# In the expert slots: h copied by DMA, transposed as float32r, and in the middle of the next first product

## The chip, the cores and the metric

The kernel runs on one core of a Trainium2 chip. Its metric is the device time of one execution in microseconds. Before the change the median of three runs is 1048.81 us (1048.38 to 1049.65). One more execution was recorded by the hardware profiler; it took 1047.6 us, and all views below are of it.

## The reference

Three stages in float32: attention with a position bias over 4 × 8 heads, a mixture of experts that sends each of 2304 tokens to one expert of eight, and a dense two-layer part. The change is in the second:

```python
N, D, E, F = (2304, 512, 8, 1024)
e_idx = np.argmax(logits, axis=1)
for e in range(E):
    mask = e_idx == e
    h = np.maximum(x[mask] @ w1[e], 0.0)
    out[mask] = gate_w[mask, None] * (h @ w2[e])
```

The third stage multiplies its (2304, 512) input by (512, 2048), applies `h * 1/(1+exp(-1.702 h))` and multiplies by (2048, 512).

## The kernel before

The attention part ends at about 340 us, the routing follows, the expert slots run from about 365 to 630 us, and the dense part to the end. A tile framework with a scheduler sets the order of the instructions on each engine from the order of the code, the buffers and its own estimates; each engine then works strictly through its queue and waits on semaphores.

Tokens are sorted by expert, and an expert slot is 128 sorted tokens of one expert. 21 slots always run; two more blocks of two stand behind a branch (`optional`, L981 and L982) and are skipped with this data. Products are made of three float32r matmuls, because each operand is split in a high part (a cast on ScalarE, names with h) and a low part (a subtraction on VectorE, names with l): high × high, high × low, low × high (`mm3`). For slot s:

- `gather` brings the 128 rows of x (`xg`), by an indirect DMA from GpSimd's queue. `load_w` brings eight pieces of the expert's weights (`wraw`) by SyncE's queue, only where the expert is new; `split_w` casts each piece on ScalarE (`wh`, L840) and subtracts on VectorE (`wl`, L842). Weight pieces are numbered 8 s to 8 s + 7: four for the first product and four for the second. There are ten buffers for each kind.
- `tx` transposes x with four float32r transposes (`turn`, L146) and splits it into `xh` and `xl` (L861, L862).
- `p1` is the first product, 24 matmuls of 128x512 (L867) in four steps k_ over two halves of h, and two ReLU activations into `h` in SBUF (L882).
- `th` transposes h, eight plain float32 transposes of 128x128 with the identity `ident` (L892), and splits it into `hh` (L894) and `hl` (L895).
- `p2_` is the second product, 24 matmuls (L867), the scaling by the gate into `y` (L908), and a store of `y` to DRAM (`Yc`, L910) from GpSimd's queue.

`run` interleaves them by slots: `p1` of slot s, `tx` of slot s+1, `p2_` of slot s−1, splits of the next weights, `th` of slot s, the rest of the splits. The first slots also carry the end of the routing (small work on all engines).

Beside the slots from 13 on, pieces 4 to 7 of the dense weights are converted in steps that `along` hands out: `conv_load` (L154 to L156) loads a raw piece `cvraw` into one of two buffers, and `conv_steps` works on it: s1 an Abs on ScalarE (L167), s2 to s4 four rows on VectorE (L171 to L181), s5 a cast on ScalarE (L188), s6 a subtraction on VectorE (L194). `conv_list` puts the load of the next piece ahead of the steps of one. The dense part's products are `f` (L1030) and `o` (L1063); the first `f` and `o` groups are worked on around the last slot, and `o` needs the converted pieces.

Of the kernel before, what the change touches and what calls it, by code (L numbers as in the profile page):

```python
# [9 lines left out]
F32 = mybir.dt.float32  # L10
F32R = mybir.dt.float32r
F16 = mybir.dt.float16
I32 = mybir.dt.int32
# [100 lines left out]
def body(ctx, tc, qk, vv, few, mid, ew1, ew2, ww, cst, alog, out, dbg=None):  # L114
    nc = tc.nc
    pe, act, dve, pool, sp = nc.tensor, nc.scalar, nc.vector, nc.gpsimd, nc.sync
# [23 lines left out]
    ident = cs[:, C_ID:C_ID + 128]  # L140
# [3 lines left out]
    def turn(out_, in_):  # L144

        pe.transpose(out_.bitcast(F32R), in_.bitcast(F32R), identr)  # L146
# [3 lines left out]
    wpool = {}  # L150
# [1 line left out]
    P = {}  # L152

    def conv_load(n):  # L154
        raw = wpool["cv"].tile([128, 1024], I32, tag="cvraw", bufs=2, name=f"cvraw{n}")
        sp.dma_start(raw, wwi[n])  # L156
        rw = raw.rearrange("p (n w) -> p n w", w=2)
        P[n] = {"L": rw[:, :, 0], "H": rw[:, :, 1]}

    def conv_steps(n):  # L160

        def s1():
            d = P[n]
            d["a"] = wpool["cv"].tile([128, 512], I32, tag="cva", bufs=1, name=f"cva{n}")
            tc.keep_in_program_order(act.activation(d["a"].bitcast(F32), d["H"].bitcast(F32), AF.Abs))  # L167

        def s2():
            d = P[n]  # L170
            dve.tensor_scalar_max(d["a"].bitcast(F32), d["a"].bitcast(F32), 2.0 ** -15)  # L171
            dve.tensor_scalar(d["a"], d["a"], 5, 2, op0=ALU.logical_shift_left, op1=ALU.logical_shift_right)

        def s3():
            d = P[n]
            dve.scalar_tensor_tensor(d["a"], in0=d["H"], scalar=-1073741824, in1=d["a"],
                                     op0=ALU.bitwise_and, op1=ALU.bitwise_or)

        def s4():
            d = P[n]  # L180
            dve.scalar_tensor_tensor(d["a"], in0=d["L"], scalar=29, in1=d["a"],  # L181
                                     op0=ALU.logical_shift_right, op1=ALU.bitwise_or)

        def s5():
            d = P[n]
            pool_ = wpool["w0"] if n % 12 < 8 else wpool["w1"]
            d["hi"] = pool_.tile([128, 512], F32R, tag=f"wh{n % 12}", name=f"wh{n}")
            act.copy(d["hi"], d["a"].bitcast(F32))  # L188

        def s6():  # L190
            d = P.pop(n)
            pool_ = wpool["w0"] if n % 12 < 8 else wpool["w1"]
            lo = pool_.tile([128, 512], F32R, tag=f"wl{n % 12}", name=f"wl{n}")
            dve.tensor_tensor(lo, d["a"].bitcast(F32), d["hi"].bitcast(F32), op=ALU.subtract)  # L194
            wt[n] = (d["hi"], lo)
        return [s1, s2, s3, s4, s5, s6]

    wwi = ww.bitcast(I32)

    def conv_list(ns, first_loaded=False):  # L200
        out_ = [] if first_loaded else [lambda: conv_load(ns[0])]
        for i, n in enumerate(ns):
            if i + 1 < len(ns):
                out_.append(lambda m=ns[i + 1]: conv_load(m))
            out_ += conv_steps(n)
        return out_
# [597 lines left out]
    def experts():  # L804
        with ExitStack() as cx:
# [5 lines left out]
            raw, wsp, xg, xt, hs, ht = {}, {}, {}, {}, {}, {}  # L811
# [34 lines left out]
            def gather(s_, last):  # L846
                if s_ >= last:
                    return
                t = xg[s_] = mp.tile([128, DM], F32, tag="xg", bufs=3, name=f"xg{s_}")
                V["gather"] = pool.indirect_dma_start(t, None, X, bass.IndirectOffsetOnAxis(ap=rt[:, s_:s_ + 1], axis=0)).ins  # L850
# [18 lines left out]
            def cols(pair, sl):  # L869
                return [t[:, sl] for t in pair]  # L870

            def p1(s_):
                ps = [one(f"p1_{s_}_{f}", "two") for f in range(2)]
                x = xt.pop(s_)
                for k_ in range(4):
                    w = wsp.pop(8 * s_ + k_)
                    a = cols(x, slice(128 * k_, 128 * k_ + 128))
                    for f in range(2):
                        mm3(ps[f], a, cols(w, slice(512 * f, 512 * f + 512)), k_ == 0, k_ == 3)
                h = hs[s_] = m1.tile([128, 1024], F32, tag="h", name=f"h_{s_}")  # L880
                for f in range(2):
                    act.activation(h[:, 512 * f:512 * f + 512], ps[f], AF.Relu)  # L882

            def th(s_):
                h = hs.pop(s_)
                hh = m1.tile([128, 1024], F32R, tag="hh", name=f"hh{s_}")
                hl = m1.tile([128, 1024], F32R, tag="hl", name=f"hl{s_}")
                for f in range(2):
                    ps = one(f"th{s_}_{f}")
                    for k_ in range(4):  # L890
                        c0 = 512 * f + 128 * k_
                        pe.transpose(ps[:, 128 * k_:128 * k_ + 128], h[:, c0:c0 + 128], ident)  # L892
                    sl_ = slice(512 * f, 512 * f + 512)
                    act.copy(hh[:, sl_], ps)  # L894
                    dve.tensor_tensor(hl[:, sl_], ps, hh.bitcast(F32)[:, sl_], op=ALU.subtract)  # L895
                ht[s_] = (hh, hl)
# [15 lines left out]
            def run(first, count, between=()):  # L912

                last = first + count
                gather(first, last)
                gather(first + 1, last)
                for n in range(6):
                    if n == 3:
                        tx(first, last, tc.keep_in_program_order)
                    split_w(8 * first + n, last)  # L920
                for s_ in range(first, last + 1):
                    gather(s_ + 2, last)
                    if s_ < last:
                        p1(s_)
                    with tc.issue_after(V["mm"]) if s_ == first else ExitStack():
                        tx(s_ + 1, last)
                    if s_ - first in between:
                        between[s_ - first]()
                    if s_ > first:
                        p2_(s_ - 1)  # L930
                    for j in range(4):
                        if s_ == first and j >= 2:
                            split_w(8 * s_ + 4 + j, last)
                        split_w(8 * (s_ + 1) + j, last)
                    if s_ < last:
                        th(s_)
                    for j in range(4, 8):
                        split_w(8 * (s_ + 1) + j, last)

# [10 lines left out]
            def rest_of_routing():  # L950
                if not last_steps:
                    last_steps.append(route_last())
                with tc.issue_after(V["gather"]), tc.issue_after(V["split"]):
                    if next(last_steps[0], "end") == "end":
                        rcx.close()

            steps = conv_list([4, 5, 6, 7])

            def along(n, *fs):
# [86 lines left out]
    def dense():  # L1046
        with ExitStack() as cx:
            wpool["w1"] = cx.enter_context(tc.tile_pool(name="w1", bufs=1))
            wpool["cv"] = cx.enter_context(tc.tile_pool(name="cv2", bufs=1))
            d2 = cx.enter_context(tc.tile_pool(name="d2", bufs=2))  # L1050
            dp = cx.enter_context(tc.tile_pool(name="dp", bufs=1))
            po = {}
# [87 lines left out]
```

## Time and profile before

| what | value |
|---|---|
| median of three runs | 1048.81 us (1048.38 to 1049.65) |
| the profiled execution | 1047.6 us, span 1046.0 us |
| PE busy | 997.0 us, 95% of the span |
| DVE busy | 753.9 us, 72% |
| ACT busy | 638.9 us, 61% |
| POOL busy | 133.7 us, 13% |
| weight splits on DVE, L842 | 167 of 1244 ns |
| weight casts on ACT, L840 | 168 of 1064 ns |

The shares are means over the attention, the slots and the dense part, which load the engines differently. A row of a timeline has its start and its duration from the profile; where instructions of one engine are pipelined, the step from one start to the next is what one costs, and it is shorter than the duration.

### The profile page before, as it was taken

What the parts mean: (1) busy time and instruction counts of PE and PEld (TensorE: products, weight loads), DVE (VectorE), ACT (ScalarE), POOL (GpSimd) and SP (SyncE); (2) the same over time, 40 slices, a digit from 0 to 9 for tenths busy, and PEclk for the clock granted to TensorE, in tenths of its full rate; (3) what the DMA queues carried; (4) which work ended last, traced back from release to release, by engine and by line L of the source; (5) the groups of instructions that cost most, each with busy time, mean ns of one, the idle gap of its engine ahead of it and who ended that gap; (6) DMA issues with size and microseconds to landing.
All of it is one profiled execution on the core that took longest, in us unless ns stands there. A gap on an engine that the chain in (4) does not pass through costs nothing. (4 is left out here: it accounts for less than half of the span.)

```text
span 1046.0 us, 16882 instructions
## 1 busy us (share of the span) xinstructions
PE 997.0 (95%) x5806; PEld 817.5 (78%) x5806; DVE 753.9 (72%) x1476; ACT 638.9 (61%) x1203; POOL 133.7 (13%) x136
## 2 busy tenths in 40 slices
PE   5799999999999499999999999999999999999997
PEld 1246777777777378888888888999989999999996
DVE  7786888788788799999999984635563666374433
ACT  7776777687777489999999973544342333232221
POOL 6410000000000344551111000000000000001212
PEclk9899999999999799999999999999999999999999
DMA  8887766776851332511261342400120111010111
GB/s 248 297 239 214 208 170 176 202 208 164 213 143 43 132 108 56 198 41 57 75 232 61 130 133 83 141 31 29 53 81 1 41 61 61 1 41 31 51 41 60
DMA packets 52058, 119.02 MB, mean 114 GB/s; under 512 B 8449, under 2 KB 17921, under 8 KB 51969
## 3 DMA queue, kind: packets, MB, share of 16 engines
q1 hardware_dynamic: 47024, 101.88, 32.9%
q0 software_dynamic: 4800, 15.73, 4.3%
q8 instruction: 47, 0.77, 0.3%
q14 instruction: 43, 0.34, 0.1%
q10 hardware_dynamic: 144, 0.29, 0.1%
HBM read 146.57 MB, written 25.84 MB: 165 GB/s over the span
## 5 line engine op out<-in xcount | busy, mean ns | idle before, releaser
L842 DVE TENSOR_TENSOR wl<-wraw,wh 128x1024 fp32r<-128x1024 f32 x167 | 198.6, 1244 | 6.7 <-ACT wh L840 4.9
L840 ACT CAST wh<-wraw 128x1024 fp32r<-128x1024 f32 x168 | 171.5, 1064 | 18.5 <-DMA wraw<-in_moe_w_dram 8.6
L1033 ACT ACTIVATE sg<-f 128x384 f32<-128x384 f32 x96 | 47.2, 491 | 177.5 <-PE f L1030 177.5
L1035 DVE TENSOR_TENSOR gg<-f,sg 128x384 f32<-128x384 f32 x96 | 53.4, 556 | 139.8 <-ACT sg L1033 139.7
L1030 PE MATMUL f<-yh,wh 128*128 128x384 f32 x384 | 129.9, 338 | 1.0 <-ACTq L982 1.0
L574 DVE CUSTOM_DVE_ANT_0 p<-sc,bias 128x576 f32<-128x576 f32 x144 | 106.3, 752 | 32.4 <-PE sc L571 31.3
L1030 PE MATMUL f<-yh,wl 128*128 128x384 f32 x384 | 129.5, 337 | 0.0
L1030 PE MATMUL f<-yl,wh 128*128 128x384 f32 x384 | 129.5, 337 | 0.0
L578 ACT ACTIVATE p<-p,mx 128x576 f32<-128x576 f32 x144 | 111.3, 774 | 20.0 <-DVE mx L574 16.4
L1063 PE MATMUL o<-wh,gl 128*128 128x512 f32 x288 | 114.0, 396 | 0.0
L1063 PE MATMUL o<-wl,gh 128*128 128x512 f32 x288 | 113.4, 394 | 0.0
L1063 PE MATMUL o<-wh,gh 128*128 128x512 f32 x288 | 113.4, 394 | 0.0
L571 PE MATMUL sc<-kk,qh 128*128 128x288 f32 x320 | 101.3, 334 | 4.1 <-ACT bev L253 1.9
L571 PE MATMUL sc<-kk,ql 128*128 128x288 f32 x320 | 88.8, 296 | 0.0
L1038 ACT CAST gh<-gg 128x384 fp32r<-128x384 f32 x96 | 49.3, 513 | 53.1 <-DVE gg L1035 52.8
L654 PE MATMUL pv<-pt,v 128*64 128x256 f32 (+2 forms) x528 | 77.5, 411 | 0.0
L1030 PEld LDWEIGHTS f<-yh,wh 128*128 128x128 f32 x384 | 72.1, 188 | 5.2 <-ACTq L982 1.4
L1039 DVE TENSOR_TENSOR gl<-gg,gh 128x384 fp32r<-128x384 f32 x96 | 53.5, 557 | 30.7 <-ACT gh L1038 30.7
L1030 PEld LDWEIGHTS f<-yl,wh 128*128 128x128 f32 x384 | 72.1, 188 | 4.1
L599 PE MATMUL tp<-cs,p 128*128 128x128 f32 x512 | 75.0, 274 | 0.2
L1030 PEld LDWEIGHTS f<-yh,wl 128*128 128x128 f32 x384 | 72.1, 188 | 0.0
L571 PEld LDWEIGHTS sc<-kk,qh 128*128 128x128 f32 x320 | 62.9, 197 | 10.4 <-ACT bev L253 3.7
(180 smaller groups left out, 2015.9 us busy)
## 6 DMA issues: line engine op xcount, KB each, us to landing
wraw<-in_moe_w_dram SPq DMA_DIRECT2D x176, 512.0 KB
cvraw<-in_ww_dram SPq DMA_DIRECT2D x32, 512.0 KB
biasD<-bev SPq DMA_DIRECT2D x36, 295.5 KB
raw<-in_qk_dram SPq DMA_DIRECT2D x16, 640.0 KB
Yc<-y POOLq DMA_DIRECT2D x21, 256.0 KB, 2.4
v<-in_vv_dram SPq DMA_DIRECT2D x16, 320.0 KB
kk<-qh SPq DMA_DIRECT2D x16, 320.0 KB
kk<-ql SPq DMA_DIRECT2D x16, 320.0 KB
```

Source lines behind the costliest of these rows:

```text
L571: pe.matmul(ps[:, hf, :288], lhsT=l_, rhs=r_[:, 288 * hf:288 * hf + 288], start=n == 0, stop=n == len(terms) - 1)
L574: dve.tensor_tensor_reduce(out=pp.rearrange("p (a j) -> p a j", a=2), in0=ps[:, :, :288], in1=bt[:, h].rearrange("p (a j) -> p a j", a=2), ...
L578: act.activation(pp, pp, AF.Exp, bias=mx[:, h:h + 1], scale=-1.0, accum_out=rs[:, c % 2, h:h + 1] if c < 4 else rs)
L599: pe.transpose(ps[:, 128 * cc:128 * cc + 128], p[:, c0:c0 + 128], ident)
L654: pe.matmul(ps[64 * h:64 * h + 64, :W], lhsT=vm[g][:, 256 * h + 64 * cc:256 * h + 64 * cc + 64], rhs=G["pt", half][:, 4 * h + cc, cols], s ...
L840: act.copy(h, t)
L842: V["split"] = by.tensor_tensor(l, t, h.bitcast(F32), op=ALU.subtract).ins
L1030: pe.matmul(ps, lhsT=w[x_][:, 128 * k_:128 * k_ + 128], rhs=y_[:, k_, :], start=k_ == 0 and n_ == 0, stop=k_ == 3 and n_ == 2)
L1035: dve.tensor_tensor(gg, ps, sg, op=ALU.mult)
L1038: act.copy(gh, gg)
L1039: dve.tensor_tensor(gl, gg, gh.bitcast(F32), op=ALU.subtract)
L1063: pe.matmul(po[t_], lhsT=a_[:, sl_], rhs=b_, start=fc == 0 and n_ == 0, stop=fc == 3 and n_ == 2)
```

## The change

`p1` gets a function that it calls when two of its four steps are through, and `run` passes one that does `th` of the slot before. `th` is no longer called behind `p2_`. Each half of h, once it is activated, is copied by a DMA from GpSimd's queue into a new tile `hd`, and `th` transposes `hd` by `turn`, as float32r, instead of h. For pieces 4 to 7 of the dense weights `cvraw` has one buffer instead of two, and each load stands directly ahead of its own steps; the dense part has two buffers again.

```diff
     def conv_load(n):
-        raw = wpool["cv"].tile([128, 1024], I32, tag="cvraw", bufs=2, name=f"cvraw{n}")
+        raw = wpool["cv"].tile([128, 1024], I32, tag="cvraw", bufs=wpool.get("cvn", 2), name=f"cvraw{n}")
...
     def conv_list(ns, first_loaded=False):
+        if wpool.get("cvn") == 1:
+            return [f for n in ns for f in [lambda m=n: conv_load(m)] + conv_steps(n)]
         out_ = [] if first_loaded else [lambda: conv_load(ns[0])]
...
-            def p1(s_):
+            def p1(s_, halfway):
                 ps = [one(f"p1_{s_}_{f}", "two") for f in range(2)]
...
                         mm3(ps[f], a, cols(w, slice(512 * f, 512 * f + 512)), k_ == 0, k_ == 3)
-                h = hs[s_] = m1.tile([128, 1024], F32, tag="h", name=f"h_{s_}")
+                    if k_ == 1:
+                        halfway()
+                h = m1.tile([128, 1024], F32, tag="h", name=f"h_{s_}")
+
+                hd = hs[s_] = m1.tile([128, 1024], F32, tag="hd", name=f"hd_{s_}")
                 for f in range(2):
                     act.activation(h[:, 512 * f:512 * f + 512], ps[f], AF.Relu)
+                    pool.dma_start(hd[:, 512 * f:512 * f + 512], h[:, 512 * f:512 * f + 512])
...
-                        pe.transpose(ps[:, 128 * k_:128 * k_ + 128], h[:, c0:c0 + 128], ident)
+                        turn(ps[:, 128 * k_:128 * k_ + 128], h[:, c0:c0 + 128])
...
+                    def halfway():
+                        if s_ > first:
+                            th(s_ - 1)
                     if s_ < last:
-                        p1(s_)
+                        p1(s_, halfway)
+                    else:
+                        halfway()
...
-                    if s_ < last:
-                        th(s_)
...
+            wpool["cvn"] = 1
             steps = conv_list([4, 5, 6, 7])
...
+            wpool["cvn"] = 2
             d2 = cx.enter_context(tc.tile_pool(name="d2", bufs=2))
```

On TensorE, in a settled slot, the transposes of slot 3's h (`th3_0` and `th3_1`) stood between the second product of slot 2 and the first product of slot 4:

```order
L867 MATMUL p2_2_5233<-wh_23_5022,hh2_5154 128x512
L867 MATMUL p2_2_5233<-wl_23_5023,hh2_5154 128x512
L867 MATMUL p2_2_5233<-wh_23_5022,hl2_5155 128x512
L892 MATMUL th3_0_5310<-cs_75,h_3_5218 128x128 x4
L892 MATMUL th3_1_5317<-cs_75,h_3_5218 128x128 x4
L867 MATMUL p1_4_0_5346<-wh_32_5270,xh4_5226 128x512
L867 MATMUL p1_4_0_5346<-wl_32_5271,xh4_5226 128x512
```

In the changed kernel, at the same place of TensorE's queue, they stand in the middle of slot 4's first product and read `hd_3`:

```order
L869 MATMUL p1_4_1_5343<-wh_33_5305,xh4_5238 128x512
L869 MATMUL p1_4_1_5343<-wl_33_5306,xh4_5238 128x512
L869 MATMUL p1_4_1_5343<-wh_33_5305,xl4_5239 128x512
L146 MATMUL th3_0_5358<-identr_77,hd_3_5228 128x128 x4
L146 MATMUL th3_1_5365<-identr_77,hd_3_5228 128x128 x4
L869 MATMUL p1_4_0_5342<-wh_34_5310,xh4_5238 128x512
L869 MATMUL p1_4_0_5342<-wl_34_5311,xh4_5238 128x512
```

The transposes moved behind half a product, with the same neighbours otherwise.

On VectorE, at the first slots, the low part of slot 0's h (`hl0`) stood behind slot 1's x and ahead of the splits of slot 1's weights (`wl_8` to `wl_15`) and of a late one of slot 0 (`wl_6`):

```order
L862 TENSOR_TENSOR xl1_4740<-tx1_4734,xh1_4739 128x512
L895 TENSOR_TENSOR hl0_4817<-th0_0_4818,hh0_4816 128x512
L895 TENSOR_TENSOR hl0_4817<-th0_1_4825,hh0_4816 128x512
L842 TENSOR_TENSOR wl_8_4769<-wraw0_4596,wh_8_4768 128x1024
L842 TENSOR_TENSOR wl_9_4792<-wraw1_4597,wh_9_4791 128x1024
L842 TENSOR_TENSOR wl_6_4797<-wraw6_4602,wh_6_4796 128x1024
L842 TENSOR_TENSOR wl_10_4802<-wraw2_4598,wh_10_4801 128x1024
L842 TENSOR_TENSOR wl_11_4812<-wraw3_4599,wh_11_4811 128x1024
L842 TENSOR_TENSOR wl_12_4833<-wraw4_4600,wh_12_4832 128x1024
L842 TENSOR_TENSOR wl_13_4838<-wraw5_4601,wh_13_4837 128x1024
L842 TENSOR_TENSOR wl_14_4843<-wraw6_4602,wh_14_4842 128x1024
L842 TENSOR_TENSOR wl_15_4848<-wraw7_4603,wh_15_4847 128x1024
```

On the same engine in the changed kernel:

```order
L864 TENSOR_TENSOR xl1_4743<-tx1_4737,xh1_4742 128x512
L844 TENSOR_TENSOR wl_8_4772<-wraw0_4596,wh_8_4771 128x1024
L844 TENSOR_TENSOR wl_9_4795<-wraw1_4597,wh_9_4794 128x1024
L844 TENSOR_TENSOR wl_6_4800<-wraw6_4602,wh_6_4799 128x1024
L844 TENSOR_TENSOR wl_10_4805<-wraw2_4598,wh_10_4804 128x1024
L844 TENSOR_TENSOR wl_11_4815<-wraw3_4599,wh_11_4814 128x1024
L844 TENSOR_TENSOR wl_12_4820<-wraw4_4600,wh_12_4819 128x1024
L844 TENSOR_TENSOR wl_13_4825<-wraw5_4601,wh_13_4824 128x1024
L844 TENSOR_TENSOR wl_14_4830<-wraw6_4602,wh_14_4829 128x1024
L844 TENSOR_TENSOR wl_15_4835<-wraw7_4603,wh_15_4834 128x1024
L902 TENSOR_TENSOR hl0_4856<-th0_0_4857,hh0_4855 128x512
L902 TENSOR_TENSOR hl0_4856<-th0_1_4864,hh0_4855 128x512
```

The two rows of `hl0` moved from ahead of the nine splits to behind them; in later slots, too, hl stands behind the eight splits of the next slot's weights.

On ScalarE at the join, ahead of the branch (`COMPARE_AND_BRANCH`), piece 7 of the dense weights had its Abs (`cva7`) and its cast (`wh7`) ahead of the last slot's result `y20`:

```order
L188 CAST wh6_7975<-cva6_7895 128x512
L1038 CAST gh0_7969<-gg0_7967 128x384
L167 ACTIVATE cva7_7979<-cvraw7_7893 128x512
L188 CAST wh7_7985<-cva7_7979 128x512
L908 ACTIVATE y20_8014<-p2_20_7989,gt_81 128x512
L981 TENSOR_LOAD fl_85
L982 COMPARE_AND_BRANCH
```

On ScalarE in the changed kernel:

```order
L1049 CAST gh0_8031<-gg0_8029 128x384
L188 CAST wh6_8036<-cva6_7956 128x512
L915 ACTIVATE y20_8077<-p2_20_8052,gt_81 128x512
L167 ACTIVATE cva7_8042<-cvraw7_8040 128x512
L992 TENSOR_LOAD fl_85
L993 COMPARE_AND_BRANCH
```

The Abs of piece 7 moved behind `y20`, and the cast of piece 7 went behind the branch.

## Rows read from the trace of the kernel before

**Rows 1.** by stretches (its length, then busy us by engine, PEclk, DMA).

```profile
474.00:498.00 24.00, 24.00 (x136) 20.09 (x135) 22.14 (x23) 21.78 (x28) 3.70 (x4) 1.00 0.21 65
```

**Rows 2.** PE, one settled slot (start, us, line, operation, out<-in, count).

```profile
419.97 0.46 PE L146 MATMUL tx<-identr,xg 128*128 128x128 f32 x4
420.27 0.47 PE L867 MATMUL p<-wh,hh 128*128 128x512 f32 x1
...
425.81 1.03 PE L892 MATMUL th<-cs,h 128*128 128x128 f32 x8
426.60 0.48 PE L867 MATMUL p<-wh,xh 128*128 128x512 f32 x1
```

**Rows 3.** PE, twelve float32r transposes in the dense part.

```profile
635.95 1.15 PE L146 MATMUL ty<-identr,yi 128*128 128x128 f32 x12
636.94 0.41 PE L1030 MATMUL f<-yh,wh 128*128 128x384 f32 x1
```

**Rows 4.** DVE, the first slots.

```profile
373.87 0.69 DVE L862 TENSOR_TENSOR xl<-tx,xh 128x512 fp32r<-128x512 f32 x1
374.48 1.28 DVE L895 TENSOR_TENSOR hl<-th,hh 128x512 fp32r<-128x512 f32 x2
375.79 12.88 DVE L842 TENSOR_TENSOR wl<-wraw,wh 128x1024 fp32r<-128x1024 f32 x9
388.60 0.68 DVE L862 TENSOR_TENSOR xl<-tx,xh 128x512 fp32r<-128x512 f32 x1
```

**Rows 5.** ACT, the first slots.

```profile
372.08 1.28 ACT L882 ACTIVATE h<-p 128x512 f32<-128x512 f32 x2
...
374.68 8.66 ACT L840 CAST wh<-wraw 128x1024 fp32r<-128x1024 f32 x9
```

**Rows 6.** PE, start of slot 2's second product.

```profile
408.08 0.46 PE L867 MATMUL p<-wh,hh 128*128 128x512 f32 x1
```

**Rows 7.** DVE, four splits in a settled slot.

```profile
430.07 4.62 DVE L842 TENSOR_TENSOR wl<-wraw,wh 128x1024 fp32r<-128x1024 f32 x4
434.61 0.68 DVE L862 TENSOR_TENSOR xl<-tx,xh 128x512 fp32r<-128x512 f32 x1
```

**Rows 8.** all stores of Yc from POOL (min/median/max ns; landing us).

```profile
L910 POOL DMA_DIRECT2D Yc<-y x21: 539/562/614, 392.2 to 631.9; - x21
...
DMA to landing us min/median/max: 2.3/2.4/5.6
```

**Rows 9.** SP's queue, the load of piece 7.

```profile
620.41 0.36 SPq L156 DMA_DIRECT2D cvraw<-in_ww_dram  x1
```

**Rows 10.** by stretches, behind that load (columns as in rows 1).

```profile
621.30:623.70 2.40, 2.40 (x18) 2.19 (x17) 1.58 (x4) 1.95 (x4) 0.39 (x1) 1.00 0.76 222
```

**Rows 11.** DVE, the first gl of the dense part.

```profile
627.18 0.55 DVE L1039 TENSOR_TENSOR gl<-gg,gh 128x384 fp32r<-128x384 f32 x1
```

**Rows 12.** PE, the first f behind the branch and the first o.

```profile
631.68 0.44 PE L1030 MATMUL f<-yh,wh 128*128 128x384 f32 x1 [1.01 <-ACTq L982]
...
633.87 0.39 PE L1063 MATMUL o<-wh,gh 128*128 128x512 f32 x1
```

**Rows 13.** ACT, y of slot 20.

```profile
630.90 0.68 ACT L908 ACTIVATE y<-p,gt 128x512 f32<-128x512 f32 x1
```

**Rows 14.** by stretches, two with a low granted clock.

```profile
27.30:34.10 6.80, 3.73 (x24) 0.78 (x24) 2.89 (x6) 3.23 (x8) 1.59 (x1) 0.50 0.91 320
...
366.00:368.00 2.00, 2.00 (x6) 1.52 (x6) 0.76 (x3) 1.04 (x1) 0.53 (x2) 0.50 1.05 411
```

**Rows 15.** PE, slot 0's first product at the low clock.

```profile
365.56 0.79 PE L867 MATMUL p<-wh,xh 128*128 128x512 f32 x1 [0.68 <-ACT xh L861]
...
367.01 0.63 PE L867 MATMUL p<-wl,xh 128*128 128x512 f32 x1
367.44 1.05 PE L867 MATMUL p<-wh,xl 128*128 128x512 f32 x2
...
368.66 0.39 PE L867 MATMUL p<-wl,xh 128*128 128x512 f32 x1
```

## The prediction

> **What bounds the kernel now.** I read the busy time by stretches first, then the engines' rows in order of time: one settled slot, the first slots, and the join to the dense part. In the settled slots TensorE is busy for 24.00 of 24.00 us, while VectorE and ScalarE have 1.9 and 2.2 us free [rows 1]. So there only what is taken off TensorE's queue counts, as long as nothing that it waits for comes late. A slot on TensorE is two products, four transposes of x and eight of h. The second product takes 425.81 − 420.27 = 5.54 us with its re-entry after transposes, x takes 420.27 − 419.97 = 0.30 and h 426.60 − 425.81 = 0.79 [rows 2]: 2 × 5.54 + 0.30 + 0.79 = 12.17 us.
>
> **Part 1: float32r transposes (a gain in 18 slots).** Eight plain transposes cost 0.79 us. Four float32r ones cost 0.30 [rows 2], twelve 636.94 − 635.95 = 0.99 [rows 3]; eight should lie between, at 0.645. From the four alone it would be 2 × 0.30 = 0.60, from the twelve 0.99 × 8/12 = 0.66. The gain is 0.145 us a slot, 0.13 to 0.19. The move itself costs TensorE nothing: there were two re-entries in a slot, behind x and behind h, and there still are two. Part 2 ends with the start of slot 2's second product; eighteen transposes of h follow it (slots 3 to 20): −2.6 us, between −2.3 and −3.4.
>
> **Part 2: the first slots (a loss).** Here VectorE's order decides. Before, hl of slot 0 stands directly behind xl1. Now it stands behind nine weight splits (wl_8 to wl_15 and wl_6), because its code now comes half a slot later. The second product of slot 0 reads hl from its third matmul on. In the trace xl1 starts at 373.87, hl at 374.48, and the nine splits run from 375.79 until xl2 starts at 388.60 [rows 4]. Without hl ahead of them they start up to 1.31 us earlier; I take 0.9, since ScalarE's first cast for them still follows its copies of h from 372.08 on and that of x [rows 5]. At the row's 388.60 − 375.79 = 12.81 us, hl of slot 0 starts at 374.9 + 12.8 = 387.7 and its first half is there at 388.3. Only then the product starts.
>
> TensorE has nothing else to do by then. Its first product of slot 1 is bound to the splits of that slot's first weights, of which the last is the fifth of the nine: 374.9 + 5 × 1.135 (below) = 380.6. Six matmuls and the routing's small ones are left, some 2 us, so from about 382.8 on it stands empty for some 5.5 us.
>
> From 388.35 on a slot takes 2 × 5.54 + 0.30 + 0.645 = 12.02 us, so the second product of slot 2 starts two slots later at 412.4, against 408.08 before [rows 6]: +4.3 us. In these two slots hl1 would be ready at about 400.2 (hl0 done 388.9, xl2 0.6, routing rows some 1.0, eight splits 9.1, half of hl 0.65), for a third matmul at 400.8; so it should not wait again. The bounds: nine splits at the settled pace, (434.61 − 430.07)/4 = 1.135 us each [rows 7], take 10.2 instead of 12.8, which gives +1.7; one split more of delay gives +5.4.
>
> **Part 3: the new dependencies in settled slots (nothing).** VectorE needs per slot 8 × 1.135, 0.61 for xl and 1.31 for hl (374.48 − 373.87 and 375.79 − 374.48 [rows 4]): 11.0 of 12.02 us. hl comes last in its slot now. Counted from the middle of the first product, where the weight buffer for the slot's eighth cast comes free (0.35 allowed until it is let go, and 8.66/9 = 0.96 for it [rows 5]), its split (1.14) and half of hl (0.65) are through at 3.1. hl is wanted after the transposes, half a product, x and two matmuls, at 0.645 + 2.77 + 0.30 + 0.46 = 4.2. The cover is 1.1 us; were a delay d beyond it, each of 18 slots would lose d.
>
> The copy of h is two more DMA issues a slot on GpSimd's queue. Its store of Yc takes 0.56 us to issue and lands 2.4 us later, 5.6 at worst [rows 8]. h is complete 1.28 us after its product [rows 5], so hd is there 1.28 + 2 × 0.56 + 2.4 = 4.8 us after it, 8.0 at worst. The transposes ask for it 0.30 + 5.54 + 2.77 = 8.6 us after it. What is queued behind the copies on GpSimd, the gather for a later slot and the next store, has most of a slot of time. Bounds: 0 and +0.5 us in the sum, for a copy or two that land late beside a load of weights.
>
> **Part 4: one conversion buffer (a loss at the join).** Before, the load of dense weight 7 is issued at 620.41 [rows 9] and moves in a stretch that ends by 623.70 [rows 10], 3.3 us later. Now it may go only when the last reader of weight 6's buffer is through, a step of VectorE behind the first gl, which the trace has from 627.18 on [rows 11]: some 628.0. It lands at 631.3. ScalarE's Abs of weight 7 stands behind y20 and ahead of its branch now, and TensorE's first f behind the branch waits for ScalarE to reach that: 631.68 in the trace [rows 12], right after y20 (630.90 + 0.68 [rows 13]). With Abs behind the load it is about 632.2. VectorE then has four steps of weight 7 left before its own branch, until 634.5, and o, at 633.87 before [rows 12], starts at about 634.7: +0.85 us. Bounds: 0 (if y20 is so late by part 2 that the load is in by then) and +2.
>
> **Part 5: the clock (a likely loss).** The empty stretch of part 2 may have a sequel. The granted clock was 0.50, which is 1.2 GHz, from 27.3 to 34.1 us, where TensorE was busy for 3.73 of 6.80, and from 366 to 368, behind a thin stretch at the routing [rows 14]. In the second case seven matmuls from 365.56 to 368.66 started up to 0.43 us apart [rows 15], against 0.23 at 2.4 GHz. If the same follows an empty 5.5 us, it is 7 × 0.2 = +1.4 us, 0 to 3.2. The Trainium skill ("TensorE: Matmul & The Clock Gate", Part 1: The HAM clock gate) says that the lower level is the default and that sustained activity releases the higher one. The trace agrees, and by that rule the fall comes with part 2's emptiness and vanishes with it.
>
> **Sum.** 4.3 − 2.6 + 0.85 + 1.4 = +3.95 us. The profiled execution took 1047.6 us (span 1046.0 and 1.6 around it), so it would be 1051.6; the median of the runs, 1048.81, is 1.2 above it. From the median: 1052.7 us.
>
> **Rivals.**
> 1. The clock does not fall in the gap. For: TensorE is full ahead of it and behind it, which it was in neither of the two falls. Against: in 5.5 us it does nothing at all. Sum +2.55, 1051.4 us.
> 2. Not slower: the nine splits run at the settled pace. For: 1.135 us each alone. Against: the row of 12.81, whose cause the change does not take away. The place is wl_8 to wl_15, the price 2.6 us; the gap is then 2.9 us, in which I expect no fall of the clock, and it decides if hl of slot 0 is through by 386: 1.7 − 2.6 + 0.85 = −0.05, 1048.8 us. With the join hidden and 0.19 a slot as well it would be 1.7 − 3.4 = −1.7, 1047.1.
> 3. hl comes late in every slot: the cover of 1.1 us is used up, because GpSimd issues three stores and copies a slot instead of one beside VectorE's splits. At 0.3 us beyond the cover 18 slots lose 5.4 more: 1058 us. Against: with one store a slot, four splits take 4.54 us [rows 7].
> 4. hd comes late, because GpSimd cannot issue while VectorE works. From the rows: held back by one split each, the copies land at 1.28 + 2 × 1.7 + 2.4 = 7.1 of 8.6 us, still hidden, and the sum stays; held back by two or more it is late by 1 us and 18 slots lose 18: 1071 us. Against: 21 issues took 539 to 614 ns [rows 8], while VectorE split for 11 of 12 us. The Trainium skill ("SBUF — State Buffer", SBUF: two separate sides) has a rule for this: a DMA from GpSimd's queue takes about 620 ns alone, but about 3100 beside a VectorE copy that holds the port which the two share. An estimate by it puts hd at 1.28 + 2 × 3.1 + 2.4 = 9.9 us, 1.3 late in each slot. The trace of the kernel before does not show this for these splits.
>
> **How the numbers follow.** The forecast has 0.48, rival 1 0.22, rival 2 0.15, rival 3 0.07, rival 4's late case 0.02; 0.06 stays for a gain that I do not see. Within 0.2%, about what a measurement of this kernel can tell from no change, is 1046.7 to 1050.9 us. The forecast's own range is 1050.6 to 1055.5, rival 1's 1049.9 to 1053. Slower: 0.46 + 0.14 + 0.09 = 0.69; same: 0.02 + 0.08 + 0.10 from rival 2 = 0.20; faster: 0.05 from rival 2's far end and the 0.06, 0.11. A range from 1047.8 to 1056 leaves out about two in ten.
>
> **What would show it.** In the changed profile: eight transposes of h that take 0.60 to 0.66 us; eighteen slots of 12.0 us; TensorE idle for about 5.5 us before 388, released by VectorE's hl; a granted clock of 0.50 for about 3 us behind it; o at the join waiting for VectorE. The prediction is wrong if that gap is under 3 us, if the clock stays up, or if TensorE waits for hl or hd in settled slots.

## The result, and the profile after

The changed kernel takes 1058.09 us (median of five runs, 1057.95 to 1060.45) against 1048.38 (five runs, 1047.42 to 1049.65): slower by 0.94%, ratio 1.0094 with a 95% interval of 1.008 to 1.0108. The forecast was 1052.7, and 1058.09 lies outside its range. The profiled executions differ by 10.3 us of span, and marks on TensorE split this into stages. "x1" is the start of slot 1's transposes of x, "p2 of slot n" the first matmul of its second product.

| stage | before, us | after, us | difference | forecast |
|---|---|---|---|---|
| start to x1 | 372.56 | 373.42 | +0.86 | 0 |
| x1 to p2 of slot 2 | 35.52 | 42.97 | +7.45 | +4.3 and +1.4 |
| p2 of slot 2 to p2 of slot 20 | 216.96 | 213.91 | −3.05 | −2.6 |
| p2 of slot 20 to the first o | 8.83 | 10.36 | +1.53 | +0.85 |
| first o to the last matmul | 403.89 | 403.98 | +0.09 | 0 |
| last matmul to the end | 8.19 | 11.63 | +3.44 | 0 |

The first row, 0.86 us, is from the start of the program to a place ahead of everything that the change touches. It varied from 371.62 to 373.89 us over the kernels below except one that adds work ahead of it, so it is no effect of the change: what stands there is the end of the routing and the rise of the granted clock, at 368.6 us before and at 370.2 after.

**First slots.** TensorE's rows in order of time (start, us, line, operation, count, idle before and releaser), from x1 on:

```profile
373.42 0.46 PE L146 MATMUL tx<-identr,xg 128*128 128x128 f32 x4
...
377.61 0.49 PE L146 MATMUL th<-identr,hd 128*128 128x128 f32 x2 [3.73 <-DMA hd<-h]
...
380.54 0.63 PE L869 MATMUL p<-wh,xl 128*128 128x512 f32 x1
...
387.49 0.40 PE L341 MATMUL gt<-r_u,r_R 128*128 128x82 f16 x6
390.71 0.76 PE L869 MATMUL p<-wh,hh 128*128 128x512 f32 x1 [2.82 <-ACT xh L863]
...
416.39 0.46 PE L869 MATMUL p<-wh,hh 128*128 128x512 f32 x1
```

Two stops stand here that the kernel before did not have, and slot 2's second product, at 408.08 in [rows 6], starts at 416.39. For 3.73 us TensorE waits for hd of slot 0, then 2.82 us ahead of slot 0's second product. The releaser named there, xh, is that of slot 2; it ended at 390.66, and this product does not read it. Of what the product reads, hl of slot 0 came last: its first half, written from 389.88 on, ended at 390.57. VectorE's rows:

```profile
375.21 0.68 DVE L864 TENSOR_TENSOR xl<-tx,xh 128x512 fp32r<-128x512 f32 x1
375.81 12.75 DVE L844 TENSOR_TENSOR wl<-wraw,wh 128x1024 fp32r<-128x1024 f32 x8
388.74 1.23 DVE L844 TENSOR_TENSOR wl<-wraw,wh 128x1024 fp32r<-128x1024 f32 x1 [0.18 <-ACT wh L842]
389.88 1.28 DVE L902 TENSOR_TENSOR hl<-th,hh 128x512 fp32r<-128x512 f32 x2
```

Against [rows 4], hl (now 389.88) stands behind all nine splits. They take 389.88 − 375.81 = 14.07 us, 1.26 more than the 12.81 of the kernel before. Most of what both have above nine times the 1.135 of [rows 7] is one split, the last in the row of eight. It runs beside the one split that GpSimd does (`wl_7`). By itself, and GpSimd's:

```profile
385.15 3.41 DVE L844 TENSOR_TENSOR wl<-wraw,wh 128x1024 fp32r<-128x1024 f32 x1
```

```profile
384.42 3.07 POOL L844 TENSOR_TENSOR wl<-wraw,wh 128x1024 fp32r<-128x1024 f32 x1 [3.68 <-ACT hh L901]
```

In the kernel before it took 3.42 us, from 382.99 on, beside GpSimd's from 382.77 on. The ninth waits 0.18 us for its cast, which waited for a buffer that the late first product of slot 1 frees; no other row of VectorE's up to hl waits for TensorE. GpSimd's queue shows why hd was not there when TensorE asked for it, at 373.9:

```profile
373.00 1.85 POOL L336 TENSOR_TENSOR r_u<-r_W,r_g 128x450 f16<-128x450 f16 x1 [4.14 <-DVE r_g L416]
374.79 1.18 POOL L889 DMA_DIRECT2D hd<-h  x2
```

h itself was complete at 374.2. A routing row (r_u) held the queue until 374.8, then the two issues took 1.18 us, and the first copy landed at 377.6. The granted clock fell behind both stops (stretch and length, busy us by engine, PEclk, DMA share, GB/s):

```profile
374.00:376.00 2.00, 0.00 (x0) 0.00 (x0) 1.93 (x6) 2.00 (x4) 1.98 (x4) 1.00 0.04 14
376.00:378.00 2.00, 0.39 (x3) 0.39 (x3) 2.00 (x2) 2.00 (x3) 1.84 (x2) 0.75 0.68 254
378.00:380.00 2.00, 2.00 (x13) 1.70 (x12) 2.00 (x3) 2.00 (x3) 1.84 (x3) 0.50 0.10 18
382.00:384.00 2.00, 2.00 (x7) 1.57 (x6) 2.00 (x2) 1.70 (x3) 0.00 (x0) 0.55 0.00 0
388.00:390.00 2.00, 0.00 (x0) 0.00 (x0) 1.82 (x3) 2.00 (x4) 1.52 (x2) 1.00 0.00 0
390.00:392.00 2.00, 1.29 (x3) 1.13 (x4) 2.00 (x6) 2.00 (x4) 1.14 (x2) 0.66 0.74 227
392.00:394.00 2.00, 2.00 (x6) 1.51 (x6) 2.00 (x4) 0.90 (x2) 0.00 (x0) 0.50 0.43 166
```

From 377.0 to 383.8 and from 390.6 to 394.1 it is at 1.2 GHz: 0.43 us a matmul, as in [rows 15], against 0.23.

**Settled slots.** The step from one slot to the next falls from 12.20 us to 12.02 (means of slots without other work in them), most of it because the eight transposes cost 0.64 us instead of the 0.79 of [rows 2]:

```profile
424.66 0.80 PE L146 MATMUL th<-identr,hd 128*128 128x128 f32 x8
425.30 0.47 PE L869 MATMUL p<-wh,xh 128*128 128x512 f32 x1
...
428.14 0.46 PE L146 MATMUL tx<-identr,xg 128*128 128x128 f32 x4
428.44 0.46 PE L869 MATMUL p<-wh,hh 128*128 128x512 f32 x1
```

**Join.** TensorE waits 2.16 us for ScalarE to reach the branch (before, 1.01, [rows 12]), then 0.20 for VectorE:

```profile
630.30 0.39 PE L869 MATMUL p<-wh,hh 128*128 128x512 f32 x1
...
638.08 0.44 PE L1041 MATMUL f<-yh,wh 128*128 128x384 f32 x1 [2.16 <-ACTq L993]
...
640.66 0.47 PE L1075 MATMUL o<-wh,gh 128*128 128x512 f32 x1 [0.20 <-DVEq L993]
```

**End.** Behind the last product stand GpSimd's last rows. The longest drain of each kernel (third number, in ns) is:

before:

```profile
L1133 POOLq DRAIN  x3: 40/115/6188, 1038.9 to 1045.7; - x3
```

after:

```profile
L1145 POOLq DRAIN  x3: 40/115/9622, 1045.8 to 1056.0; - x3
```

It is 3.43 us longer, with 102 transfers issued from GpSimd's queue instead of 60. Behind it only the closing semaphores of all engines are left, so the span is longer by as much.

### The profile page after: what moved, and what is told of

Its sections match the earlier page's. It is cut to its first block, busy times and chain, and to the rows that moved or that the text cites. A ratio compares the mean times of both kernels' runs of the same rounds, so it can differ in the third digit from the quotient of the medians.

```text
span 1056.3 us, 16997 instructions
## 1 busy us (share of the span) xinstructions
PE 998.1 (94%) x5806; PEld 817.4 (77%) x5806; DVE 752.8 (71%) x1476; ACT 640.6 (61%) x1203; POOL 157.1 (15%) x178
## 5 line engine op out<-in xcount | busy, mean ns | idle before, releaser
L1085 POOL DMA_INDIRECT out_dram<-acc,ot x18 | 18.1, 1006 | 391.4 <-DVE gl L1050 326.0
```

## The experiments

**1. Copies without a reader (copies42).** Kernel before, one conversion buffer, and in `p1`:

```diff
+                hd = m1.tile([128, 1024], F32, tag="hd", name=f"hd_{s_}")
                 for f in range(2):
                     act.activation(h[:, 512 * f:512 * f + 512], ps[f], AF.Relu)
+                    pool.dma_start(hd[:, 512 * f:512 * f + 512], h[:, 512 * f:512 * f + 512])
```

> The kernel before, with one conversion buffer for pieces 4 to 7, and with the 42 copies of h into hd from GpSimd's queue, which nobody reads: the transposes stay plain, on h and at their old place. Theory A (GpSimd's last row, a drain that took 6.19 us before and 9.62 after, grows with the transfers issued from its queue, 60 before and 102 after): drain 9.6 us, time before + 3.4 for it and + 0 to 1 at the join, 1052 to 1053. Rival B (the longer drain belongs to something else in the changed kernel, such as its longer code): drain 6.2 us, time 1048.4 to 1049.4. Either way the first slots should be as before, with slot 2's second product within 1 us of 408.

```profile
L1139 POOLq DRAIN  x3: 40/115/9620, 1040.6 to 1050.8; - x3
```

The drain is 9.62 us, as in the changed kernel, with TensorE's order of the kernel before: rival B falls. From x1 to p2 of slot 2 it is 35.49 us, as before; join 9.91. Time 1054.28, ratio 1.0049 (1.0032 to 1.0066): above the 1052 to 1053 that were expected. The profiled execution took 1052.71, and its stages add up to that; what the median has beyond it is not explained.

**2. Half as many issues (copies21).** `pool.dma_start(hd, h)` once a slot, behind both halves.

> As the kernel with 42 unread copies, but with one copy of 512 KB a slot instead of two of 256: 21 more issues, the same bytes and packets. If theory A holds by the number of issues, the drain is 6.19 + 21 x 3.43/42 = 7.9 us; if it holds by packets or bytes, 9.6 us; by rival B 6.2 us. The time follows: before + 1.7, + 3.4 or + 0, and 0 to 1 at the join.

```profile
L1139 POOLq DRAIN  x3: 40/115/7907, 1039.3 to 1047.8; - x3
```

7.907 us is what the count of issues gives (7.9): 60, 81 and 102 transfers from GpSimd's queue have drains of 6.19, 7.91 and 9.62, which is 0.082 us each, whether they are of 256 or of 512 KB. Time 1051.31, ratio 1.0031 (1.0017 to 1.0044).

**3. The copies from ScalarE's queue (actq).** In the changed kernel `pool.dma_start` becomes `act.dma_start`.

> The changed kernel with its 42 copies of h issued from ScalarE's queue instead of GpSimd's. Theory A: drain back at 6.2 us, so 3.4 less than after at the end. Theory C (the first slots lose because TensorE stops at the transposes of slot 0 until hd has landed, the clock falls in that stop, and hl of slot 0 then comes behind nine splits): a copy from another queue changes little of it, the stop is 2 to 4 us, slot 2's second product starts at 414 to 417, time about 1054.5. Rival D (the stop is GpSimd's own: its copy waited for the routing's r_u ahead of it): the stop is under 2 us, the clock stays up, slot 2's second product starts by 413, time about 1051.

```profile
L1145 POOLq DRAIN  x3: 40/115/6188, 1051.0 to 1057.8; - x3
```

The drain is back at 6.19: theory A holds. The stop for hd is 2.04 us instead of 3.73, so GpSimd's own share was 1.7, but x1 to p2 of slot 2 still takes 42.30; rival D falls. The time that TensorE no longer waits for hd it waits for hl instead (xh in the second row is again that of slot 2, which the product does not read; hl's first half, from 389.67 on, came last of what it reads):

```profile
376.39 0.54 PE L146 MATMUL th<-identr,hd 128*128 128x128 f32 x4 [2.04 <-DMA hd<-h]
...
390.50 0.66 PE L869 MATMUL p<-wh,hh 128*128 128x512 f32 x1 [4.79 <-ACT xh L863]
```

2.04 + 4.79 = 6.83 us here, 3.73 + 2.82 = 6.55 in the changed kernel: the stop for hd lies inside the time in which VectorE has not come to hl yet. The time, 1059.69 (ratio 1.0112, 1.007 to 1.0154), is 5 us above what theory C gave, and the new loss is ScalarE's. Its rows around two copies in a late slot:

```profile
612.69 1.08 ACT L888 ACTIVATE h<-p 128x512 f32<-128x512 f32 x2
613.32 1.13 ACTq L889 DMA_DIRECT2D hd<-h  x2
614.49 0.59 ACT L863 CAST xh<-tx 128x512 fp32r<-128x512 f32 x1 [0.71 <-ACT h L888]
```

The cast of x waits behind the issues (0.71 us idle), later casts follow late, and hl with them: slots 2 to 20 take 216.83 us, so that the gain of 3.05 is gone, and the join 12.34.

**4. The move alone (moveplain).** Changed kernel without hd, `turn` back to `pe.transpose(..., h, ident)`, two conversion buffers.

> The move alone: transposes of h in the middle of the next first product, but plain, on h itself; no hd, no copies, two conversion buffers as before. Here the written order puts hl of slot 0 ahead of the nine splits again. Theory C: without a copy to wait for, the first slots lose nothing; slot 2's second product starts at 408 to 409, settled slots take 12.17 us, drain 6.2 us, time 1048 to 1049.5. Rival E (the move by itself costs the first slots their time, as the prediction has it): slot 2's second product at 412 or later, time 1052 or more.

Slot 2's second product starts at 413.03, 39.68 us behind x1, which is 4.16 more than before: rival E has it, theory C falls in this form. Settled slots take 12.20 us and the drain 6.19. The time is 1052.87 (ratio 1.0039, 1.0025 to 1.0053). TensorE's row:

```profile
401.23 0.50 PE L869 MATMUL p<-wh,hl 128*128 128x512 f32 x1 [2.54 <-DVE hl L899]
```

VectorE's rows, seven of the splits of slot 2's weights (one stands ahead of them) and then hl:

```profile
392.55 8.03 DVE L844 TENSOR_TENSOR wl<-wraw,wh 128x1024 fp32r<-128x1024 f32 x7
400.50 1.28 DVE L899 TENSOR_TENSOR hl<-th,hh 128x512 fp32r<-128x512 f32 x2
```

hl of slot 0 is early here. It is hl of slot 1 that stands behind eight splits of slot 2's weights, four more than before, and the third matmul of its product stops for 2.54 us. With its re-entry this stop makes 2.98 of the 4.16 us; the other 1.18 arise ahead of slot 1's second product, and which row makes them was not taken apart. So the move costs about 4 us without any copy, most of it by VectorE's order; which slot's hl carries it depends on the order.

**5. Slot 0 as before (old0).** Transposes of slot 0 plain and at the old place.

```diff
+                        if s_ > first and s_ - 1 >= 1:
+                            th(s_ - 1)
...
+                    if s_ < min(last, 1):
+                        th(s_)
```

> The changed kernel, with the transposes of slot 0 alone at their old place and plain on h; 40 copies from GpSimd's queue for slots 1 to 20. hl of slot 0 stands ahead of the nine splits again and nothing waits for hd of slot 0, but hl of slot 1 still stands behind all eight splits of slot 2's weights. Theory C2 (two causes of about 4 us each: the stop for hd of slot 0 with the fall of the clock, and hl behind splits in the first two slots, where VectorE has no slack yet): slot 2's second product 4 us after that of the kernel before, 412 to 413; slots 2 to 20 gain 3.0, the join loses 1 to 1.5, the drain 3.3: before + 5.5 to 6, 1054. Rival F (all the loss hangs on slot 0: its hd and its hl): second product of slot 2 at 408 to 409, time 1050 to 1051.

x1 to p2 of slot 2: 38.42 us, +2.9 (411.94 in all). VectorE writes hl of slot 1 from 399.58 on, behind eight splits, and the third matmul of its product starts at 400.33, as it can. The clock was low from 390.4 to 397.2 here, behind stops of 0.30 and 1.12 us, but TensorE would have waited for hl anyway. Rival F falls; theory C2's second half is nearer 3 than 4. Time 1053.47, ratio 1.005 (1.0033 to 1.0067).

**6. Slots 0 and 1 as before (old01, old01_again).** The same with 2 for 1.

> As the kernel with slot 0 alone at the old place, but slots 0 and 1 both at their old place and plain; 38 copies. hl of slot 1 stands behind four splits, as before the change. Theory C2: slot 2's second product at 408 to 409, 18 slots gain 3.0 us after it, join 1 to 1.5, drain 38 x 0.082 = 3.1 us: before + 1 to 2, 1049.5 to 1050.5. Rival F: the same as with slot 0 alone, 1050 to 1051, within 0.7 us of it. If VectorE's lag only moves on to hl of slot 2, its second product stops at its third matmul by 1 us or more.

In the profiled execution (1052.56 us) p2 of slot 2 starts at 408.30 as C2 has it, 36.57 behind x1, +1.05. The loss moves on: ScalarE's casts stop TensorE for 1.86 us, and slot 2's step is 14.20. The other four executions took 1062.8 to 1066.4 (over all five the ratio is 1.017, 1.0153 to 1.0187), which nothing above explains, so the kernel was run once more:

> The same kernel as old01 once more, for a profile of another execution: of its five executions one took 1052.6 us, the profiled one, and four 1062.8 to 1066.4. If the long ones belong to it, this one shows where 13 us go. Theory: hd of some slot lands late when it meets a load of weights, TensorE stops for it and its clock falls, at two or three places of 4 to 6 us. Rival: no place at all, but a low clock over a long stretch.

It took 1067.44 us, and one place has it. TensorE:

```profile
430.95 0.72 PE L146 MATMUL th<-identr,hd 128*128 128x128 f32 x4 [10.88 <-DMA hd<-h]
```

GpSimd:

```profile
413.64 10.39 POOL L852 DMA_INDIRECT xg<-X,rt  x1 [0.17 <-issue]
424.04 1.11 POOL L890 DMA_DIRECT2D hd<-h  x2
```

VectorE at the same time:

```profile
413.92 9.17 DVE L844 TENSOR_TENSOR wl<-wraw,wh 128x1024 fp32r<-128x1024 f32 x8
```

A gather of x, which takes 0.95 to 1.89 us in the kernel before, lasted 10.39 us here. It ended 0.94 us behind eight splits that VectorE ran without a gap for 9.17 us. hd of slot 3 was queued behind the gather. That is not all of the stop: the first copy was issued at 424.04, and its landing ended the stop 6.9 us later, beside weight loads that kept the DMA engines busy (share 0.98 to 1.02 from 424 to 430); the median from issue to landing is 2.6 us. In the other profile the same gather fell on a different moment of VectorE's work:

```profile
409.10 1.62 POOL L852 DMA_INDIRECT xg<-X,rt  x1 [0.16 <-issue]
```

That points to rival 4's mechanism, for a gather and not on every execution; no run took VectorE's work away to show it, and gathers of the kernel before that ran beside two splits without a gap took 1.5 to 1.8 us. The Trainium skill's rule ("SBUF — State Buffer", SBUF: two separate sides), that GpSimd cannot write a transfer's descriptors while VectorE holds the port they share, is for VectorE operations in a 2-port mode, such as a copy. The splits are subtractions with two inputs, for which that section names only GpSimd operations that read SBUF. The issues of the 42 copies of the changed kernel took 536 to 622 ns beside splits. What held this gather and not those is not settled here.

**7. The other half alone (oldplace).** All transposes at the old place, as float32r on hd, 42 copies from GpSimd.

> The other half of the change alone: all transposes of h at their old place, but as float32r on hd, 42 copies from GpSimd's queue, one conversion buffer. hl of slot 0 stands behind two splits, hl of slot 1 behind four. Theory C2: TensorE still stops about 3.7 us for hd of slot 0 and the clock falls, so slot 2's second product is 3 to 4.5 us later than before, 411 to 412.5; 18 slots gain 3.0, join 1 to 1.5, drain 3.4: before + 5 to 6, 1054. If hd is late in settled slots at the old place (4.8 us needed, 5.84 there), TensorE's transposes wait for it, and the gain goes. Rival F2 (the stop alone, without the late hl, is made up for by VectorE's lag): second product of slot 2 within 1 us of before, time 1050.

```profile
PE th L146 <- DMA hd<-h: 9.3, 10, 2.4
```

TensorE waits for hd in ten transposes, 9.3 us in all, and with the clock's falls it costs more: x1 to p2 of slot 2 41.03 us (+5.5), one later slot step 16.24. The stops of slots 0 and 1 (2.36, 0.22 and 0.50 us) and a fall of the clock make 1.5 of the 5.5; that of slot 2 (2.00 us and a fall of the clock) makes 4.0, and it does not occur where the transposes stand in the middle of the next product. Time 1063.48, ratio 1.0145 (1.0129 to 1.0162). The gain needs the middle of the next product, where 8.6 us are left for the copy; the old place leaves 5.8.

**8. One copy from SyncE, old place, spread conversion (best_spread).** Slots 0 and 1 plain; `sp.dma_start(hd, h)`; the steps of pieces 4 to 7 two a slot.

> A version that keeps the gain and drops the three losses: all transposes at their old place, slots 0 and 1 plain on h, slots 2 to 20 as float32r on hd, one copy of 512 KB a slot, issued from SyncE's queue instead of GpSimd's; one conversion buffer, with the conversion steps of pieces 4 to 7 spread evenly over slots 13 to 20. Theory A and C2: drain 6.19 us, slot 2's second product at 408 to 408.5, 18 slots gain 2.6 to 3.0, join 0 to +0.7: 1045.5 to 1046.5, faster than before by 2 to 3 us. Rival: SyncE's queue holds the copies behind loads or the loads behind copies, and TensorE waits in settled slots for hd or wh: no gain, 1048 or more. Rival: the conversion steps in settled slots make hl late, since VectorE has some 1 us free a slot: 18 slots lose what they gained from slot 13 on.

```profile
PE th L146 <- DMA hd<-h: 7.9, 3, 3.3
```

```profile
546.00:558.00 12.00, 9.89 (x45) 7.98 (x44) 10.07 (x12) 8.56 (x12) 1.56 (x2) 0.86 0.77 298
```

Time 1057.78, ratio 1.009 (1.0073 to 1.0107): the first of its rivals. Where weights are loaded (DMA share 0.77 over this stretch) hd comes late behind them: three stops, 7.9 us in all, each with a fall of the clock. The first of them is slot 2's, so that its second product starts at 413.64 instead of 408 to 408.5. The drain is 6.19, and the join 8.98 us: with the steps spread, one buffer costs 0.15.

**9. The order on VectorE without a stop (fill).** In the changed kernel, behind slot 1's x and ahead of slot 0's second product:

```diff
+                    for i in range(13):
+                        tc.keep_in_program_order(pe.matmul(fill, lhsT=identr, rhs=h, start=True, stop=True))
...
+                    for i in range(12):
+                        tc.keep_in_program_order(pe.matmul(fill, lhsT=identr, rhs=h[0][:, :512], start=True, stop=True))
```

> The changed kernel with 25 matmuls of 512 columns added on TensorE that nobody reads: 13 behind the transposes of slot 1's x and 12 ahead of slot 0's second product. They hold the clock up in the two stretches where it fell, and with them slot 0's transposes stand in the middle of slot 1's first product, so TensorE doesn't stop for hd either; hl of slot 0 still stands behind the nine splits. This is part 2 of the prediction by itself. Theory C2 (7.45 us lost between the transposes of slot 1's x and slot 2's second product: about 4.2 by VectorE's order, the rest by the stop and the clock): 39.5 to 40.3 us between these two, against 35.5 before and 43.0 after; time after - 3, 1055. Rival G (the late hl came only from the stop and the low clock): 37 us or less. Rival H (all of it is VectorE's order, stop and clock are hidden behind it): 42.5 to 43.

VectorE's splits and hl, TensorE's second added row and the product, then two stretches with the clock (columns as above):

```profile
379.58 11.98 DVE L844 TENSOR_TENSOR wl<-wraw,wh 128x1024 fp32r<-128x1024 f32 x8 [0.26 <-ACT wh L842]
...
392.86 1.28 DVE L906 TENSOR_TENSOR hl<-th,hh 128x512 fp32r<-128x512 f32 x2
```

```profile
389.03 3.04 PE L914 MATMUL fill_b<-hh,identr 128*128 128x512 f32 x12
393.60 0.50 PE L873 MATMUL p<-wh,hh 128*128 128x512 f32 x1 [1.53 <-DVE hl L906]
```

```profile
384.00:388.00 4.00, 4.00 (x24) 3.31 (x23) 4.00 (x4) 3.62 (x5) 0.56 (x1) 1.00 0.03 10
388.00:392.00 4.00, 4.00 (x35) 3.15 (x33) 3.84 (x3) 1.36 (x2) 3.84 (x2) 1.00 0.00 0
```

x1 to p2 of slot 2 takes 40.37 us, +4.85, with the clock at 1.00 and no stop for hd. VectorE's nine splits (379.58 to 392.86) and hl behind them set the start of slot 0's second product. The first thirteen added matmuls take 3.1 us, nearly as long as the stop for hd: the run takes the low clock away, not TensorE's delay. Its stages beside those of the changed kernel and of actq:

| | after | actq | fill |
|---|---|---|---|
| stop for hd of slot 0, us | 3.73 | 2.04 | 0 |
| stop ahead of slot 0's second product | 2.82 | 4.79 | 1.53 |
| x1 to that product | 17.29 | 16.61 | 16.27 |
| that product to p2 of slot 2 | 25.68 | 25.69 | 24.10 |

The last line gives the clock: 1.6 us, behind the stop for hl. The line above it follows VectorE and not the stop for hd; most of the 1.0 us between after and fill is in the nine splits, 14.07 against 13.28 us. So of the 7.45 us of the changed kernel about 5.9 are VectorE's order, 4.85 of them in this run, and 1.6 the low clock behind the stop for hl. The stop for hd and the low clock behind it are hidden. Rival G falls, and rival H too, by the 1.6. Time 1056.84 (ratio 1.0076, 1.0056 to 1.0096), less gain than forecast: in the profiled execution slot 0's first product had begun 3.3 us later (369.15), ahead of the added work.

**10. One conversion buffer alone (cvn1).** Kernel before with the buffers and the list of the changed one.

> The kernel before with one conversion buffer for pieces 4 to 7, and nothing else: part 4 of the prediction by itself. From the start of slot 20's second product to the first o it took 8.83 us before and 10.36 after. Theory: 9.7 to 10.0 here, + 0.9 to 1.1, as with the unread copies; drain 6.19 us; time before + 1, 1048.5 to 1049.5. If the join costs 1.5 with the buffer alone, 10.3; if it is the copies that delay it, 8.8 and no change in time.

```profile
625.02 0.39 PE L869 MATMUL p<-wh,hh 128*128 128x512 f32 x1
...
632.47 0.45 PE L1033 MATMUL f<-yh,wh 128*128 128x384 f32 x1 [1.82 <-ACTq L985]
...
635.04 0.47 PE L1067 MATMUL o<-wh,gh 128*128 128x512 f32 x1 [0.21 <-DVEq L985]
```

The join takes 10.02 us, +1.2. The time, 1049.44 (ratio 1.0007, 0.9992 to 1.0023), agrees with +1.2 and with no change; the profile shows the wait (1.82 us, [rows 12] had 1.01).

**11. The version that they point to (late6).** Slots 0 to 5 as before, from 6 on in the middle, one copy a slot from GpSimd, spread conversion.

> The version that the runs so far point to: slots 0 to 5 as before the change (old place, plain), from slot 6 on transposes as float32r in the middle of the next first product, one copy of 512 KB a slot from GpSimd's queue (15 copies), one conversion buffer with the steps spread over slots 13 to 20. Gain 14 x 0.17 = 2.4 us; drain 15 x 0.082 = 1.2; join 0.15; no loss in the first slots. Sum -1.0: 1047 to 1047.5, which is within what can be told from no change. If the passage from the old to the new place costs at slot 6 what it cost at slot 1 or 2 (2 to 3 us, since VectorE and ScalarE have to be half a slot ahead), it is 1049 to 1051.

Time 1048.37 against 1047.84, ratio 0.9996 (0.9985 to 1.0008): no difference from the kernel before, 10 us better than the changed one. x1 to p2 of slot 2 takes 35.52 us, the passage at slot 6 costs nothing, the join takes 8.71, the drain 7.42 (+1.23), slots 2 to 20 215.31 (−1.65; one slot with weights arriving gives 0.7 back). Their sum is −0.5; from the first o to the last matmul 0.8 come back, where TensorE waits 0.57 us for VectorE (at 636.10), so that the stages come to +0.3, which runs cannot tell from nothing.

## Why the prediction was wrong

**The end (the step that failed most).** The sum put the copy's two issues a slot at "0 and +0.5 us", for copies that land late. It counted them while they run, not after. GpSimd's drain behind the last product grows by 0.082 us for each transfer that its queue issued: +3.44, a third of the loss and more than half of the 6.4 us by which the sum fell short of the profiled difference (runs 1 to 3). The row was in the trace of before (6.19 us, of the 8.19 behind the last matmul), and the prediction asked nowhere what stands behind the last product.

**The first slots, VectorE's order (a term too small).** Right in mechanism: hl of slot 0 stood behind nine splits, and TensorE waited for it. The size was 4.3; the move alone cost 4.16 (moveplain), the order with a full clock 4.85 (fill), and in the changed kernel it was about 5.9. The sum took the nine splits at the 12.81 us of the kernel before; they took 14.07, and hl started 16.5 us behind x1 instead of 15.1. The reason that the sum gave for the order is incomplete. It was not only that the code comes half a slot later: in moveplain, with the code at the same place and no copy, the scheduler leaves hl of slot 0 ahead of the nine splits, and the loss moves to hl of slot 1. In the changed kernel hl of slot 1 is in time, as the sum held.

**The first slots, hd and the clock.** Part 2 did not ask what slot 0's transposes, at the head of TensorE's queue, wait for. They stopped it for 3.73 us, so that the one empty stretch of 5.5 us became two, 3.73 and 2.82. The sum came to little harm by that: the first stop lies within the time that VectorE needs to come to hl (actq, fill). It was luck that the missed dependency stood behind a longer one. Part 5 had the clock fall once, after the wait for hl, for +1.4; it did, for +1.6, and the other fall, behind the stop for hd, is hidden. Rival 1, in which it stays up, fell. By the prediction's own sign, a gap under 3 us, the 2.82 count against it.

**Settled slots.** −3.05 against −2.6, inside its bounds of −2.3 to −3.4. Neither hl nor hd came late in them (no wait of TensorE from p2 of slot 2 to the join), so rival 3 fell for this kernel, and so did rival 4's late case. That rival 3 names 1058 us, the time that was measured, is chance; in actq, where casts were delayed, hl was late by 0.1 to 0.3 us in some slots, which is how small the cover is.

**The join.** +1.53 against +0.85, within its bounds of 0 to 2. Of it 1.14 stand ahead of the first f, where TensorE waits for ScalarE's branch (the sum had 0.5), and 0.39 ahead of o. One buffer alone makes 1.2. The rest may be the order of steps around hl20 in this kernel; that was not tried.

**Rival 2** did not happen: the nine splits took 14.1 us, not 10.2. Why the nine are slower than four in a settled slot, which the prediction left open, is seen in the rows of both kernels: one of them runs beside GpSimd's split and takes 3.4 us. No run took GpSimd's split away.

## What to carry to other kernels

Before pricing a new transfer, look at what its queue does after the last one: here each issue from GpSimd cost 0.082 us at the very end, however well it was hidden, so the two copies a slot (0.164) spent all of the 0.17 us that they gained, and one larger copy would have spent half. A stage that is settled says little on how the change behaves in the first slots, where the helper engine is the one behind: read its order there row by row, and ask of each row at the head of a queue what it waits for. Do not add up the waits that an engine meets in turn: here a stop of 3.73 us cost next to nothing, because what the engine needed afterwards came later still. A transfer queued behind another on GpSimd inherits that one's worst case, and one profile need not show it.

## What the runs showed of the hardware that was not expected

- GpSimd's closing drain: 6.19, 7.42, 7.91 and 9.62 us for 60, 75, 81 and 102 transfers issued from its queue, 0.082 us each, the same for copies of 256 and 512 KB.
- One subtraction of 128x1024 on VectorE took 3.4 us instead of 1.1 beside GpSimd's own of the same shape, in the kernel before, the changed one and fill.
- A gather on GpSimd lasted 10.39 us instead of 1 to 2 beside eight splits of VectorE's without a gap, in one profiled execution out of two of the same kernel; the cause is open. Beside the shortest one, the executions of that kernel are 10 to 15 us longer.
- The granted clock fell to 1.2 GHz after stops of 3.73 and 2.82 us on an otherwise busy TensorE, for 6.8 and 3.4 us. The length of a stop alone does not tell: the clock also fell behind stops of 0.30 and 1.12 us (old0, for 6.8 us) and of 1.23 and 0.33 (best_spread, for 3.4), but not behind 1.24 and 0.33 in the kernel before, nor behind 2.54 in moveplain.
